# Moving two opening loads to other queues (f_logit's first block to ScalarE's, lower_bound to GpSimd's), and what is made from one of them to a later place

**Chip, cores, metric.** One core of one Trainium2 chip. The time is the device time of one execution in microseconds (us); lower is better. "Span" is the time from the first to the last instruction in the trace of one profiled execution.

## The reference

A gated recurrence over the sequence, then a two-layer block with g(h) = h - tanh(h):

```python
sig = 1.0 / (1.0 + np.exp(-f_logit))
f = lower_bound[None, None, :] + (1.0 - lower_bound[None, None, :]) * sig
i = 1.0 - f
for t in range(S):                      # S = 6080, B = 4, D = 256
    h = f[:, t] * h + i[:, t] * x[:, t]
    y[:, t] = h
h = y.reshape(B * S, D) @ w_in          # w_in 256 x 2048, w_out 2048 x 256
out = (h - np.tanh(h)) @ w_out          # weights arrive as float64
```

## The kernel before

The sequence is cut into blocks (block 0 has 256 tokens, the others 512). Every engine's instructions stand in a fixed order, written as words. The body is full of work for TensorE (PE); the change touches only the opening. There the words mean: `W.i` load weights i (raw float64, `W.0` and `W.1` are the halves of the first weights), `df.j`/`dx.j` load block j of f_logit/x, `tf`/`tx` transpose it on PE, `sg` sigmoid on ScalarE, `f0`/`f1` make the decay on ScalarE, `v0`/`v1` make the input on VectorE, `sc0`/`sc1` the scan on VectorE (its result is y), `ce cr cx cm cs cb cw` turn weights into float32 (`cr`, `cx` on ScalarE, the rest on VectorE), `F.j.u.s` a product of the first layer, `K1.n` 2n filler matmuls on zeros, which are meant to keep PE's clock up.

```python
before = """
    K1.7 df.0 ce.0 cr.0 dx.0 cm.0 tf.0 cx.0 W.1 cs.0 tx.0 sg0.0 cb.0 K1.4
    sg1.0 df.1 v0.0 f0.0 cw.0 f1.0 v1.0 dx.1 ce.1 tf.1 sc1.0 cx.1 sc0.0 W.2 cr.1
    cm.1 tx.1 sg1.1 cb.1 sg0.1 cs.1 F.0.0.0 f0.1 v1.1 f1.1 dx.2 v0.1 K1.4 cw.1
    t.0.0.0 sc0.1 q.0.0.0 F.0.0.1 w.0.0.0 W.3 sc1.1 cr.2 K1.2 a.0.0.0 t.0.0.1
    F.1.0.0 ...                                             # cut
"""
with tc.manual_schedule():
    nc.vector.memset(zeros[:], 0.0)
    nc.vector.memset(ones[:], 1.0)
    open_by(["W.0"])                    # one half on SyncE's queue, one on ScalarE's
    nc.scalar.dma_start(out=lb[:], in_=lower_bound.rearrange("(p k) -> p k", k=KC))
    make_identity(nc, ident[:])         # GpSimd; the transposes need it
    nc.scalar.activation(out=flag[:], in_=ones[0:1, :], func=AF.Sigmoid)
    nc.scalar.activation(out=om[:], in_=lb[:], func=AF.Identity, scale=-1.0, bias=1.0)
    nc.scalar.activation(out=nom[:], in_=lb[:], func=AF.Identity, bias=-1.0)
    busy = ps_b.tile([P, TB], FP32, name="B", tag="B")
    open_by(before.split())
    ...                                                     # cut: the body
```

## Time and profile before

| | before |
|---|---|
| time, median of 3 runs | 2330.19 us (2329.85 to 2331.65) |
| span of the profiled execution | 2328.7 us |
| PE / VectorE / ScalarE busy | 2319.0 / 2122.2 / 1802.3 us |
| PE idle before 11.92 us, after 2322.8 us, between | 3.84, 5.9, 0 us |

PE is never idle in the body, so the time is the opening, plus a body of fixed length, plus a tail. These lines of the timeline (start, duration, engine, line of the kernel, instruction; in brackets the idle time before it and what ended it) hold waits:

```profile
6.25 0.67 PE L673 MATMUL Qa<-ident,fn 128*128 128x128 f32 x2 [1.38 <-DMA fn<-in_f_logit_dram]
...
11.92 0.72 PE L673 MATMUL Qc<-ident,xn 128*128 128x128 f32 x4 [0.24 <-DVE e L160]
...
13.23 0.75 DVE L694 SCALAR_TENSOR_TENSOR v<-fT,om,Qd 128x512 f32<-128x512 f32 x1 [0.83 <-PE Qd L673]
```

The first is PE's first real work, the second the first transpose of x block 1, the third VectorE's first step on block 1, for which it idles 0.83 us. The list of issues (last column: us from issue to landing) has four of the five small loads of the opening (the other half of the weights, on SyncE's queue, is left out):

```profile
raw<-in_moe_w_in_dram ACTq DMA_DIRECT2D x1, 256.0 KB, 4.3
fn<-in_f_logit_dram SPq DMA_DIRECT2D x1, 256.0 KB, 4.7
xn<-in_x_dram SPq DMA_DIRECT2D x1, 256.0 KB, 4.9
lb<-in_lower_bound_dram ACTq DMA_DIRECT2D x1, 1.0 KB, 4.3
```

### The profile page before, as it was taken

To read this page: it belongs to the slowest core of one execution; us is meant where nothing else is said; L and a number is where in the kernel's file an instruction comes from. 1 tells how busy PE (TensorE), PEld (TensorE's weight loads), DVE (VectorE), ACT (ScalarE), POOL (GpSimd) and SP (SyncE) were. 2 spreads that over 40 slices of the span, in tenths; PEclk is the share of its full clock that TensorE was granted. 3 is DMA by queue.
4 is the path that set the end of the run, shared out by engine and by line. 5 is a ranking of instruction groups with operands and counts; after the bars stand their busy time and mean duration, and the time that the engine had idled before them with its cause. 6 is when DMAs were issued, how large, how long until landed. Compare 5 with 4: busy or idle time off the path is not lost.

```text
span 2328.7 us, 28694 instructions
## 1 busy us (share of the span) xinstructions
PE 2319.0 (100%) x10693; PEld 2027.1 (87%) x10693; DVE 2122.2 (91%) x2451; ACT 1802.3 (77%) x2688; POOL 0.7 (0%) x6
## 2 busy tenths in 40 slices
PE   9999999999999999999999999999999999999998
PEld 6888888888888888888888888888888888888887
DVE  8999899998999989999999999999899998999988
ACT  7677777777777777787777777777777777777775
POOL 0000000000000000000000000000000000000000
PEclk9999999999999999999999999999999999999999
DMA  6311211111111111112111121111211112111101
GB/s 172 64 23 33 41 37 28 28 37 37 37 28 28 38 36 37 28 28 42 32 37 28 28 45 29 37 28 28 45 29 37 28 28 46 31 34 28 28 10 28
DMA packets 296943, 85.00 MB, mean 37 GB/s; under 512 B 289888, under 2 KB 292704, under 8 KB 296800
## 3 DMA queue, kind: packets, MB, share of 16 engines
q1 hardware_dynamic: 296512, 82.87, 17.1%
q8 instruction: 84, 1.38, 0.3%
q14 instruction: 59, 0.48, 0.1%
q10 hardware_dynamic: 288, 0.26, 0.1%
HBM read 58.20 MB, written 24.90 MB: 36 GB/s over the span
## 4 chain that ended last, share of the span: by engine, by line
PE 99%; DVE 0%; DMA 0%; ACT 0%; issue 0%; ACTq 0%
PE A L392 27%; PE Qa L475 14%; PE Qb L475 14%; PE D L392 14%; PE Qd L475 14%; PE Qc L475 7%; PE B L392 7%; PE Qa L795 1%; PE Qc L795 1%; PE Qb L795 1%; PE A L728 1%; PE D L728 0%; PE Qd L728 0%; PE B L728 0%; DMA lb<-in_lower_bound_dram 0%; PE A L561 0%
## 5 line engine op out<-in xcount | busy, mean ns | idle before, releaser
L392 PE MATMUL A<-T,w_in 128*128 128x256 f32 x2208 | 558.8, 379 | 0.0
L392 PEld LDWEIGHTS A<-T,w_in 128*128 128x128 f32 x2208 | 419.5, 190 | 57.0
L436 DVE TENSOR_TENSOR h<-h,q 128x1024 f32<-128x1024 f32 x368 | 437.5, 1220 | 3.1
L430 DVE SCALAR_TENSOR_TENSOR q<-q,t 128x1024 f32<-128x1024 f32 x368 | 440.1, 1216 | 0.0
L423 ACT ACTIVATE q<-t 128x1024 f32<-128x1024 f32 x368 | 382.8, 1053 | 46.6 <-DVE h L436 43.7
L420 ACT ACTIVATE t<-h 128x1024 f32<-128x1024 f32 x368 | 388.7, 1057 | 3.1 <-DVE h L407 0.3
L441 ACT ACTIVATE junk<-t 128x1024 bf16<-128x1024 f32 x368 | 388.2, 1055 | 1.5
L455 DVE TENSOR_TENSOR Tg<-h 128x1024 f32<-128x1024 f32 x368 | 348.0, 946 | 6.4
L475 PE MATMUL Qb<-h,w_out 128*128 128x256 f32 x1472 | 347.7, 379 | 0.0
L475 PEld LDWEIGHTS Qb<-h,w_out 128*128 128x128 f32 x1472 | 279.7, 190 | 38.0
L475 PE MATMUL Qa<-Tg,w_out 128*128 128x256 f32 x736 | 219.0, 379 | 0.0
L475 PE MATMUL Qa<-h,w_out 128*128 128x256 f32 x736 | 218.9, 379 | 0.0
L475 PE MATMUL Qd<-h,w_out 128*128 128x256 f32 x732 | 217.7, 379 | 0.0
L475 PE MATMUL Qd<-Tg,w_out 128*128 128x256 f32 x732 | 217.7, 379 | 0.0
L404 ACT COPY h<-B 128x512 f32<-128x512 f32 x184 | 107.0, 582 | 142.8 <-PE B L392 94.1
L404 ACT COPY h<-A 128x512 f32<-128x512 f32 x184 | 107.1, 582 | 136.6 <-PE A L392 125.2
L407 DVE TENSOR_TENSOR h<-D,r 128x512 f32<-128x512 f32 x184 | 126.9, 689 | 92.7 <-PE D L392 89.1
L407 DVE TENSOR_TENSOR h<-A,r 128x512 f32<-128x512 f32 x184 | 126.3, 686 | 73.7 <-PE A L392 42.1
L404 ACT COPY r<-A 128x512 f32<-128x512 f32 x184 | 107.3, 583 | 105.7 <-PE A L392 105.7
L392 PE MATMUL D<-y,w_in 128*128 128x256 f32 x736 | 188.9, 379 | 0.0
L392 PE MATMUL B<-y,w_in 128*128 128x256 f32 x736 | 188.9, 379 | 0.0
L392 PE MATMUL A<-y,w_in 128*128 128x256 f32 x736 | 188.9, 379 | 0.0
(136 smaller groups left out, 3077.0 us busy)
## 6 DMA issues: line engine op xcount, KB each, us to landing
xn<-in_x_dram SPq DMA_DIRECT2D x184, 128.0 KB, 3.2
fn<-in_f_logit_dram SPq DMA_DIRECT2D x184, 128.0 KB, 3.1
out_dram<-osb SPq DMA_DIRECT2D x180, 128.0 KB, 2.8
raw<-in_moe_w_out_dram SPq DMA_DIRECT2D x8, 512.0 KB, 4.8
raw<-in_moe_w_in_dram SPq DMA_DIRECT2D x7, 512.0 KB, 5.2
out_dram<-osb SPq DMA_DIRECT2D x3, 256.0 KB, 3.9
fn<-in_f_logit_dram SPq DMA_DIRECT2D x1, 512.0 KB, 7.1
xn<-in_x_dram SPq DMA_DIRECT2D x1, 512.0 KB, 8.0
```

The costliest lines, as they stand in the source:

```text
L392: nc.tensor.matmul(ps[:, c], lhsT=w_in[u][:, slot, c * P : (c + 1) * P], rhs=mixes[j][right], start=start and c == 0, stop=True, skip_grou ...
L404: nc.scalar.copy(out=dst, in_=piece(n, bank))
L407: nc.vector.tensor_tensor(out=piece(n, "h")[:, q], in0=piece(n, bank), in1=piece(n, r), op=ALU.add)
L420: nc.scalar.activation(out=half(n, i, "t"), in_=half(n, i), func=AF.Square)
L423: nc.scalar.activation(out=half(n, i, "q"), in_=half(n, i, "t"), func=AF.Square, scale=RA, bias=RB,)
L430: nc.vector.scalar_tensor_tensor(out=q, in0=q, scalar=RC, in1=t, op0=ALU.add, op1=ALU.mult)
L436: nc.vector.tensor_tensor(out=h, in0=h, in1=q, op=ALU.mult)
L441: nc.scalar.activation(out=junk[:, :, :, 0 : st[n]["hb"]], in_=t, func=AF.Relu, bias=-TINY, accum_out=flags[:, 2 * n + i : 2 * n + i + 1],)
L455: nc.vector.tensor_tensor(out=o, in0=a, in1=b, op=ALU.subtract)
L475: nc.tensor.matmul(acc[j, part][:, r, 0 : st[n]["hb"]], lhsT=w_out[u][:, slot, c * P : (c + 1) * P], rhs=piece(n, right)[:, q, c], start=( ...
L728: nc.tensor.matmul(h[c], lhsT=w_in[u][:, 2 * k + s, c * P : (c + 1) * P], rhs=ys[j][:, k, 0:nb], start=k == 0 and (c == 0 or len(banks) == 2),
L795: nc.tensor.matmul(acc[j][i // 2][:, i % 2].rearrange("p (k m) -> p k m", k=2), lhsT=plain[j, u][:, s, c, i * P : (i + 1) * P], rhs=w_out[ ...
```

## The change

The intent: SyncE's queue issues six loads one after the other, so take one off it; and ScalarE waits for lower_bound (to make om and nom) before it may turn to the first weights, so load that elsewhere and make om and nom later.

```diff
-        def load(j, s):
+        def load(j, s, queue=nc.sync):
             nat = spot(j, ("fn", "xn")[s])
-            nc.sync.dma_start(
+            queue.dma_start(
 ...
-            K1.7 df.0 ce.0 cr.0 dx.0 cm.0 tf.0 cx.0 W.1 cs.0 tx.0 sg0.0 cb.0 K1.4
+            K1.7 ce.0 cr.0 dx.0 cm.0 tf.0 cx.0 L W.1 cs.0 tx.0 sg0.0 cb.0 K1.4
 ...
             open_by(["W.0"])
-            nc.scalar.dma_start(
+            nc.gpsimd.dma_start(
                 out=lb[:], in_=lower_bound.rearrange("(p k) -> p k", k=KC)
             )
+            load(0, 0, nc.scalar)
             make_identity(nc, ident[:])
 ...            # om and nom: from here into the word L, behind cx.0
```

## The prediction

> **What bounds the kernel now.** I read the page first. PE is busy for 2319.0 of 2328.7 us, at full granted clock:
>
> ```profile
> PE 2319.0 (100%) x10693; PEld 2027.1 (87%) x10693; DVE 2122.2 (91%) x2451; ACT 1802.3 (77%) x2688; POOL 0.7 (0%) x6
> PE   9999999999999999999999999999999999999998
> ```
>
> So 9.7 us of the span are idle on PE. I looked for them in the timeline. Before 12 us PE waits four times (1.70, 1.38, 0.52 and 0.24 us, together 3.84), and its last matmul ends at 2322.8, which leaves 5.9 us of tail. 3.84 + 5.9 is already 9.7: between 11.9 and 2322.8 us PE has no hole. What shifts PE's first real work shifts the end by the same amount, and what doesn't shift it is worth nothing. The change touches only the first microseconds, so the question is what releases PE at 11.92 us. Second view, the chain of waits followed back from the end, in its first 40 us:
>
> ```profile
> 1.41 4.25 DMA lb<-in_lower_bound_dram
> 5.69 0.03 ACT om L934
> 5.98 0.58 ACT r L146
> 6.59 0.69 DVE r L157
> ...
> 11.20 0.61 DVE e L160
> 11.92 0.72 PE Qc L673 x4
> 12.64 0.48 PE Qd L673 x4
> 13.12 1.73 PE A L728 x8
> ```
>
> This looks like an invitation: the chain begins with the 1 KB load of lower_bound, which the change takes away. But its step from "DVE e L160" to "PE Qc" is doubtful. In the program, that PE instruction (the first transpose of x block 1) waits for the DMA of x block 1 and for VectorE's earlier reads of bank Qc, not for e. So, third view, the transfers: the issue in the timeline (first two lines; start, duration), and time to landing in the list of issues.
>
> ```profile
> 3.15 0.59 SPq L659 DMA_DIRECT2D fn<-in_f_logit_dram  x1
> 3.78 0.53 SPq L659 DMA_DIRECT2D xn<-in_x_dram  x1
> 10.43 0.77 PE L673 MATMUL Qa<-ident,fn 128*128 128x128 f32 x4 [0.52 <-ACT e L149]
> ...
> fn<-in_f_logit_dram SPq DMA_DIRECT2D x1, 512.0 KB, 7.1
> xn<-in_x_dram SPq DMA_DIRECT2D x1, 512.0 KB, 8.0
> ```
>
> fn block 1 lands at 3.15 + 7.1 = 10.25, and PE starts its transposes at 10.43. xn block 1 lands at 3.78 + 8.0 = 11.78, and PE goes on at 11.92. Both releases are landings; the engines named merely ended at about the same time (e at 11.80). Fourth view, busy times by microsecond (last three columns: clock, DMA share, GB/s):
>
> ```profile
> 4.00:5.00 1.00, 0.87 (x5) 0.30 (x2) 0.00 (x0) 0.00 (x0) 0.00 (x0) 1.00 1.07 357
> 7.00:8.00 1.00, 1.00 (x7) 0.93 (x6) 0.99 (x3) 0.97 (x4) 0.00 (x0) 1.00 1.02 314
> 10.00:11.00 1.00, 0.57 (x4) 0.60 (x5) 1.00 (x3) 0.94 (x2) 0.00 (x0) 1.00 1.08 379
> ```
>
> The DMA engines are full from about 2.5 us until past the last packet of xn block 1. The opening is bound by bytes: 0.5 MB weights, 0.25 f, 0.25 x, 0.5 weights, 0.5 f, 0.5 x, together 2.5 MB, must have moved before PE can go on.
>
> **What the Trainium skill says.** "DMA: Bandwidth & Descriptors", section "Issuing engines are not separate DMA queues": transfers from SP, ACT and GpSimd run on the same 16 engines and interleave, so a second issuer saves only sequencer time. The trace agrees so far as it goes: each issue costs SP 0.4 to 0.66 us, while the engines are full. The same page, "Queues, rings and completion order": each DMA engine takes turns between the rings that hold work, packet by packet. In this trace, ACT's and SP's halves of the first weights end close together (landing 4.3 and 4.5 us after the same issue time, 0.99). The same page, "Specifications": about 1 us to the first byte by GpSimd's path against 0.6 by the others; no GpSimd transfer is in this trace. "TensorE: Matmul & The Clock Gate", Part 1: PE is cold at first and becomes fast after a busy window of some 3.4 us, free-running. The trace agrees in kind: block 0's transposes take 0.31 us each, block 1's 0.16.
>
> **The change, part by part.**
>
> 1. *SP's queue.* One issue of 0.44 us goes; those of xn 0, W.1, fn 1 and xn 1 start some 0.5 us earlier (xn 1 at about 3.3 in place of 3.78). Its packets then wait longer in a ring whose engines are full; bytes ahead of them are the same 2.0 MB. Landing of xn 1: 11.8 as before. Worth 0 (at most 0.1).
>
> 2. *fn 0 on ACT's queue.* Before, it went ahead of xn 0 in one ring: landings 1.45 + 4.7 = 6.15 and 1.94 + 4.9 = 6.84. Now the two are in two rings and share the engines by turns, so I expect both near 6.6 to 6.8: fn 0 some 0.5 us later, xn 0 unchanged. PE's first transposes begin at about 6.75 in place of 6.25, the first sigmoid at 7.45 in place of 6.97, the first v at 8.3 in place of 7.89. VectorE's run to the end of cs.1 moves from 12.40 to about 12.85. The next VectorE step, v of block 1, waits for PE until 13.23 (0.83 us idle before). So 0.45 is taken from a slack of 0.83: cost on the path 0.
>
> 3. *lower_bound on GpSimd's queue.* On ACT it landed at 1.41 + 4.25 = 5.66, because its tiny packets stood behind the weights. In a ring of its own it should land between 3 and 5. The identity, behind it on GpSimd, ends at 1.55 now and an estimated 1 us later, long before 6.2. Packets and bytes are about the same: 0.
>
> 4. *om and nom behind cx.* They held ACT from 5.69 to 5.89; without them r starts when the weights land, 5.57 as VectorE's e does: 0.3 us earlier. But ACT's sum until the sigmoid is the same, so at best it gains 0.1 there. VectorE's r starts at 6.35 in place of 6.59, e 0.25 earlier, w_in (8.29) with them or after v. The first product needs w_in, the scans (end 10.88) and x 1 transposed (13.12): the last decides. Off the path: 0.
>
> Sum: 0 from each, with at most 0.1 to 0.2 us of luck either way. 2330.19 becomes about 2330.0; the 0.2 is my allowance for the issues that come earlier.
>
> **Rivals.**
>
> A. *The chain is right and lower_bound is on the path.* Then r's 0.3 us go right through: 2329.9. For it: the chain view. Against it: the landing of xn 1 at 11.78, and 0.83 us of idle VectorE later, so VectorE can't have been the bound.
>
> B. *Earlier issue does bring earlier landing* (all SP transfers by up to 0.5 us). PE could then start block 1's transposes at 9.9 and lose its 0.52 and 0.24 idle: 2329.5. For it: the engines move only 154 GB/s in the microsecond from 2 to 3. Against it: that is latency on engines already occupied (share 0.94), not a lack of issued work.
>
> C. *Sharing delays fn 0 by over 0.9 us*, or lower_bound comes late (after 6.8). Then VectorE's slack is used up and the delay beyond it reaches the path: a few tenths, 2330.5.
>
> D. *The clock gate.* A later fn 0 lengthens PE's idle time from 1.38 to about 1.9 us. If the busy window is missed, the transposes and first products (some 2.5 us of work) run at half speed: up to 2 us, 2332. Against it: the filler matmuls that follow keep PE busy from 6.75 to 10.4, as now.
>
> **Range and chances.** The three runs of before span 1.8 us (2329.85 to 2331.65), which is more than each effect here; a median of three should move by some 0.7 to either side. I predict 2330.0 with 2328.9 to 2331.3: the lower end is B plus noise, the upper C or D in part. 2% would be 47 us, four times all that happens before PE starts. Chances: faster by over 2% 0.005, within 2% 0.99, slower 0.005.
>
> **What would show it.** Right: xn 1 lands within 0.2 of 11.8, PE's x-transposes start within 0.2 of 11.92, fn 0 lands later than 6.15, r starts about 5.57, VectorE still idles before v of block 1, and PE has no hole after 12 us. Wrong: the x-transposes start at 11.5 or earlier (A or B), or after 12.2, with a longer idle ended by something of block 0 (C), or block 1's transposes at 0.3 us each (D). A time outside the range with the first 12 us unmoved would mean that something in the body changed, for which I see no cause.

## The result, and the profile after

| | before | after |
|---|---|---|
| median of 6 runs each, same rounds | 2330.1 us (2328.41 to 2331.65) | 2329.64 us (2329.47 to 2330.7) |
| span of the profiled execution | 2328.7 | 2329.0 |

The ratio is 0.9999, 95% interval 0.9986 to 1.0011: the same. (Ratios here are the mean time of one kernel's fast runs over that of the other's of the same rounds, so not quite the ratio of the medians.)

The busy line of the page is unchanged but for PE, and the chain of waits of the kernel after now starts with f_logit's first block:

```profile
PE 2319.5 (100%) x10693; PEld 2028.2 (87%) x10693; DVE 2122.2 (91%) x2451; ACT 1802.4 (77%) x2688; POOL 1.4 (0%) x7
```

```profile
1.41 5.10 DMA fn<-in_f_logit_dram
...
8.61 1.71 PE B L900 x8
10.31 0.85 PE Qa L673 x4
11.17 0.85 PE Qb L673 x4
12.02 0.77 PE Qc L673 x4
12.79 0.46 PE Qd L673 x4
13.25 1.73 PE A L728 x8
```

The first product (A, last line) starts at 13.25 in place of 13.12 in this chain (its own records start at 13.09 and 12.96; starts of the first product below are of this second kind). But the way there is another one: PE no longer waits for block 1's data at all; from 6.65 on it is busy without a hole, with fillers (B) and with transposes that take 0.85 us for four where they took some 0.6. Why, the issues and the timeline of the kernel after show:

```profile
fn<-in_f_logit_dram SPq DMA_DIRECT2D x1, 512.0 KB, 7.1
xn<-in_x_dram SPq DMA_DIRECT2D x1, 512.0 KB, 8.0
fn<-in_f_logit_dram ACTq DMA_DIRECT2D x1, 256.0 KB, 5.1
xn<-in_x_dram SPq DMA_DIRECT2D x1, 256.0 KB, 4.8
lb<-in_lower_bound_dram POOLq DMA_DIRECT2D x1, 1.0 KB, 5.3
```

```profile
3.26 0.87 SPq L659 DMA_DIRECT2D xn<-in_x_dram  x1
...
5.34 0.68 ACT L146 ACTIVATE r<-raw 128x512 f32<-128x512 uint32 x1 [1.92 <-DMA raw<-in_moe_w_in_dram]
6.65 0.68 PE L673 MATMUL Qa<-ident,fn 128*128 128x128 f32 x2 [1.78 <-DMA fn<-in_f_logit_dram]
6.76 0.20 ACT L908 ACTIVATE om<-lb 128x2 f32<-128x2 f32 x1 [0.22 <-DMA lb<-in_lower_bound_dram]
8.30 0.48 DVE L694 SCALAR_TENSOR_TENSOR v<-fT,om,Qc 128x256 f32<-128x256 f32 x1 [0.80 <-PE Qc L673]
11.82 0.97 PE L673 MATMUL Qc<-ident,xn 128*128 128x128 f32 x4
13.36 0.75 DVE L694 SCALAR_TENSOR_TENSOR v<-fT,om,Qd 128x512 f32<-128x512 f32 x1 [0.55 <-PE Qd L673]
```

x block 1 landed at 3.26 + 8.0 = 11.23 (the landing itself is in the trace's semaphore records), 0.56 us earlier than in the trace of before. PE could not use it, for two reasons: block 0's transposes began 0.4 us later, so the eight fillers behind them ran until 10.3; and PE's clock, which the trace records as fast from 10.70 us on before, became fast only at 12.57 here. That looks like my rival B (earlier landing) and my rival D (late clock) at the same time, cancelling each other. Is that what the change does, or one execution's luck? That is what the experiments are for.

### The profile page after: what moved, and what is told of

It reads as the page before. It is cut to its first block, busy times and chain, and to the rows that moved or that the text cites. A ratio compares the mean times of both kernels' runs of the same rounds, so it can differ in the third digit from the quotient of the medians.

```text
span 2329.0 us, 28694 instructions
## 1 busy us (share of the span) xinstructions
PE 2319.5 (100%) x10693; PEld 2028.2 (87%) x10693; DVE 2122.2 (91%) x2451; ACT 1802.4 (77%) x2688; POOL 1.4 (0%) x7
## 4 chain that ended last, share of the span: by engine, by line
PE 99%; DMA 0%; DVE 0%; ACTq 0%; issue 0%
PE A L392 27%; PE Qa L475 14%; PE Qb L475 14%; PE D L392 14%; PE Qd L475 14%; PE B L392 7%; PE Qc L475 7%; PE Qb L795 1%; PE Qa L795 1%; PE Qc L795 1%; PE A L728 1%; PE D L728 0%; PE Qd L728 0%; PE B L728 0%; DMA fn<-in_f_logit_dram 0%; PE B L900 0%
## 5 line engine op out<-in xcount | busy, mean ns | idle before, releaser
L392 PE MATMUL D<-T,w_in 128*128 128x256 f32 x736 | 188.9, 379 | 0.0
```

The costliest lines, as they stand in the source:

```text
L392: nc.tensor.matmul(ps[:, c], lhsT=w_in[u][:, slot, c * P : (c + 1) * P], rhs=mixes[j][right], start=start and c == 0, stop=True, skip_grou ...
```

## The experiments

Two theories. **Theory 1**: the change really brings x block 1 earlier, and the late transposes and the cold clock give it back. **Theory 2** (first a rival, "luck", then a theory of its own): the landing and the clock's step differ from one execution to the next by more than the change moves them. The table has the trace of each kernel run, times in us from the start of the span. "Marker" is the start of the filler group between the second and the third product: what comes behind it is the same in all kernels. "Tail" is from the start of the last matmul to the landing of the last output.

| trace | x block 1 lands | clock fast | marker | tail | span |
|---|---|---|---|---|---|
| before | 11.79 | from 10.70 | 17.29 | 5.06 | 2328.7 |
| before_again | 11.22 | from 9.70 | 16.72 | 5.38 | 2328.4 |
| after | 11.23 | from 12.57 | 17.42 | 5.17 | 2329.0 |
| after_again | 11.67 | 4.61 to 11.44, from 14.85 | 18.53 | 5.04 | 2329.9 |
| fn_act | 11.37 | 4.82 to 11.65, from 15.06 | 18.47 | 5.04 | 2329.8 |
| lb_pool | 12.17 | from 13.74 | 18.36 | 4.95 | 2329.7 |
| bare | 11.52 | from 14.44 | 18.37 | 5.39 | 2330.1 |
| fill_before | 11.34 | from 4.47 | 16.84 | 4.15 | 2327.5 |
| fill_after | 11.67 | from 5.97 | 17.17 | 4.33 | 2327.9 |
| late_f | 12.29 | 6.22 to 9.64, from 13.05 | 20.49 | 4.14 | 2330.9 |
| late_f2 | 11.31 | from 6.22 | 18.46 | 4.13 | 2328.9 |
| place_fill | 11.98 | from 6.98 | 17.48 | 4.14 | 2327.9 |
| fill_before2 | 11.90 | from 7.19 | 17.40 | 4.32 | 2328.0 |
| fill_after2 | 11.23 | from 5.52 | 16.73 | 4.36 | 2327.5 |

The first four experiments ran on one chip, the eight others on a second; the kernel before had a median of 2330.8 to 2330.9 us on both. (Its runs are pooled by chip: nine for the first four experiments, nine for the next four, and the same nine with one more for the last four.)

Take the landing from the marker. In before, in before_again and in the five traces named fill or place_fill, what is left is 5.50 us: there the landing alone sets the marker. In after and lb_pool it is 6.19, in bare 6.85, in after_again 6.86 and in fn_act 7.10: this excess, 0.7 to 1.6 us, is what a late PE and a slow clock cost. (In late_f and late_f2 something else is in charge, see there.)

### before_again: the kernel before, unchanged

> The kernel before, unchanged, timed against itself. Theory 1 (two changes that cancel: with the change the transfers really land earlier, and PE loses it again to a late first transpose and a cold clock): x block 1 lands near 11.8 us again (11.6 to 12.0), and the DMA engines move 280 to 340 GB/s between 5.5 and 8.5 us again. Rival (the earlier landing in the trace after was luck of one execution): x block 1 lands anywhere from 11.2 to 11.8 here. Both: the ratio is 1.000, single runs spread over 1 to 3 us, and the time at which PE's clock becomes fast differs from the 10.70 us of the first trace by up to 3 us.

Measured: 2330.74 us (2329.41 to 2331.61) beside 2330.81 of the kernel before, ratio 1.0. x block 1 landed at 11.22, as early as in the trace after, without any change. Theory 1 wanted 11.6 to 12.0, and 280 to 340 GB/s between 5.5 and 8.5 us; it was 349 here, 300 in before. So the 0.56 us need not be an effect of the change: the unchanged kernel shows as much between two executions. The 16 DMA engines were about fully occupied in both traces (a share of 1.00 and 1.02), so a full share is not a fixed rate. The issues of before_again (512 KB lines, 6.6 and 7.4 in place of 7.1 and 8.0) say the same:

```profile
fn<-in_f_logit_dram SPq DMA_DIRECT2D x1, 512.0 KB, 6.6
xn<-in_x_dram SPq DMA_DIRECT2D x1, 512.0 KB, 7.4
```

### after_again: the changed kernel, unchanged

> The changed kernel, unchanged. Theory 1: x block 1 lands at 11.1 to 11.4 us again and 355 to 390 GB/s flow between 6 and 8.5 us. Rival: it lands anywhere from 11.2 to 11.8. Both: the ratio is between 0.9990 and 1.0005; f block 0 lands at 6.4 to 6.7 and lower_bound after 6 us; PE's clock becomes fast somewhere between 10 and 13.5 us, not at 12.57 as in the first trace, and the first product starts between 12.3 (fast early) and 13.3 (fast late).

Measured: 2330.71 us (2329.12 to 2331.48), ratio 0.9998. Here PE's clock did something that neither trace had shown. The timeline of after_again, PE alone:

```profile
7.25 0.40 PE L673 MATMUL Qd<-ident,xn 128*128 128x128 f32 x2
7.50 1.04 PE L900 MATMUL B<-zeros 128*128 128x256 bf16 x8
10.31 0.71 PE L673 MATMUL Qa<-ident,fn 128*128 128x128 f32 x4 [1.77 <-DMA fn<-in_f_logit_dram]
...
11.80 1.10 PE L673 MATMUL Qc<-ident,xn 128*128 128x128 f32 x4 [0.30 <-DMA xn<-in_x_dram]
12.70 1.06 PE L673 MATMUL Qd<-ident,xn 128*128 128x128 f32 x4
13.55 2.54 PE L728 MATMUL A<-y,w_in 128*128 128x256 f32 x8
```

The clock was fast early (the eight fillers took 1.04 us; 1.91 in the traces before and after). Therefore they ended early, PE idled 1.77 us, the clock fell at 11.44, and the first product ran at half speed: 2.54 us where it took 1.89. The clock column of the busy times by stretch (third from the end) shows the fall; the rows are 7 to 8, 11 to 12 and 13 to 14 us:

```profile
7.00:8.00 1.00, 1.00 (x11) 0.94 (x10) 0.66 (x3) 1.00 (x4) 0.00 (x0) 1.00 1.00 320
11.00:12.00 1.00, 0.69 (x6) 0.53 (x5) 1.00 (x2) 0.40 (x1) 0.00 (x0) 0.72 1.04 384
13.00:14.00 1.00, 1.00 (x6) 0.91 (x5) 0.13 (x1) 1.00 (x2) 0.00 (x0) 0.50 1.37 187
```

My expectation had the first product at 12.3 to 13.3 and the clock between 10 and 13.5; both missed. So did theory 1's 355 to 390 GB/s between 6 and 8.5 us (336) and its landing at 11.1 to 11.4 (11.67). In the table, every step of the clock within a trace is a multiple of 3.41 us from the next; where that grid lies differs between executions.

### fn_act: f_logit's block alone is moved

```diff
-            nc.gpsimd.dma_start(out=lb[:], ...)
             load(0, 0, nc.scalar)
+            nc.scalar.dma_start(out=lb[:], ...)
```

> The changed kernel, but lower_bound goes back to ScalarE's queue, behind f block 0. So f block 0 alone is moved. Theory 1, if the move of f is what makes the landings earlier: x block 1 lands at 11.1 to 11.4 us. If the move of lower_bound's 128 small packets is the cause: it lands near 11.8. Rival (luck): either, without pattern. lower_bound should land near 6 to 6.6 us. Ratio 0.9990 to 1.0010.

Measured: 2331.52 us (2329.48 to 2331.67), ratio 1.0002; x block 1 at 11.37, f block 0 already at 5.67, the clock fast at 4.82 and fallen at 11.65, as in after_again. lower_bound landed at 6.80, later than my 6 to 6.6. The landing of x block 1 fits the first theory's number, but lies within the spread of the unchanged kernel. (The edits of fn_act and lb_pool are against the changed kernel, those of bare, late_f and late_f2 against the kernel before or fill_before.)

### lb_pool: lower_bound alone is moved

```diff
-            K1.7 ce.0 cr.0 dx.0 ... cx.0 L W.1 ...
+            K1.7 df.0 ce.0 cr.0 dx.0 ... cx.0 L W.1 ...
-            load(0, 0, nc.scalar)
```

> The changed kernel, but f block 0 goes back to SyncE's queue. So lower_bound alone is moved (and what is made from it stands behind the first weights' steps). Theory 1 with f as the cause: x block 1 lands near 11.8 us and f block 0 at 6.1; with lower_bound's packets as the cause: 11.1 to 11.4. lower_bound lands at 6 to 7 us as in the trace after, if GpSimd's queue as such is late, or at 3 to 5 if it was two busy rings that held it. Ratio 0.9990 to 1.0010.

Measured: 2330.77 us (2330.22 to 2331.23), ratio 1.0. x block 1 landed at 12.17, the latest of the first six traces, and f block 0 at 5.38. lower_bound landed at 1.48 + 4.1 = 5.6, neither at my 3 to 5 nor at 6 to 7. Neither part of the change moves the time by more than its spread.

### fill_before and fill_after: enough fillers to hold the clock

If the clock causes the spread, more fillers should narrow it.

```diff
-            K1.7 ...  sg0.0 cb.0 K1.4
+            K1.12 ... sg0.0 cb.0 K1.10
```

> The kernel before with 24 filler matmuls in place of 14 ahead of block 0's transposes, and 20 in place of 8 behind them. Theory 2 (the spread between executions comes from where PE's clock steps fall, in a grid of 3.41 us, and from the landing of x block 1): PE has no idle stretch over 1 us after 1.7, so the clock becomes fast between 5.1 and 8.6 us and stays fast; PE goes on within 0.2 us of each landing; the first product starts 1.0 to 1.2 us after x block 1 has landed, at 12.3 to 13.2 us; span = that start + 2315.7 (from the traces so far). Ratio 0.9994 to 0.9999, and the single runs lie within 1 us of each other where the kernel before spreads over 2 to 3. Rival (the clock is no part of it): same as before, first product at 12.4 to 14 as until now, same spread.

> The changed kernel with the same fillers. Theory 2: as fill_before, the same time as it within 0.4 us (the change moves no landing of x block 1); a consistent gain of 0.4 us or more over fill_before would say that the change does bring x block 1 earlier and the clock had hidden it.

Measured: fill_before 2329.59 us (2328.99 to 2329.97), fill_after 2329.32 (2328.5 to 2329.42), the kernel before on the same chip 2330.91 (2328.94 to 2331.61); ratios 0.9995 and 0.9992, both intervals with 1 inside. The spread fell from 2.7 us (nine runs) to 1.0 and 0.9 (five runs each), and the clock stayed fast from 4.47 (just before my 5.1 to 8.6) and 5.97 us on. In the later call, below, the spreads were 1.5 and 1.3: still narrower, but less so. The timeline of fill_before, PE alone, shows cleanly what the prediction had read in the trace of before, that both releases of PE are landings:

```profile
6.99 2.35 PE L899 MATMUL B<-zeros 128*128 128x256 bf16 x20
10.03 0.72 PE L673 MATMUL Qa<-ident,fn 128*128 128x128 f32 x4 [0.70 <-DMA fn<-in_f_logit_dram]
11.47 0.72 PE L673 MATMUL Qc<-ident,xn 128*128 128x128 f32 x4 [0.24 <-DMA xn<-in_x_dram]
12.51 1.89 PE L728 MATMUL A<-y,w_in 128*128 128x256 f32 x8
```

The first product starts 1.17 us after x block 1's landing in both traces (11.34 and 12.51; 11.67 and 12.84). But my span formula (that start + 2315.7) gives 2328.2 for fill_before, and the span was 2327.5. The difference is not in the body: from the start of the last filler to the start of the last matmul it is 2304.91 to 2305.07 us in all fourteen traces. It is in the tail. With the old number of matmuls a fetch of instructions falls beside the last output transfers; with the fillers it doesn't. The transfers at the end, first of before (from 2322 us on), then of fill_before, from 2321 us on (queue, packets, MB, share; then the last outputs, last column us to landing):

```profile
q1 hardware_dynamic: 544, 0.52, 19.5%
q8 instruction: 1, 0.02, 1.2%
...
out_dram<-osb SPq DMA_DIRECT2D x2, 256.0 KB, 4.0
```

```profile
q1 hardware_dynamic: 544, 0.52, 17.2%
q14 instruction: 3, 0.02, 0.8%
...
out_dram<-osb SPq DMA_DIRECT2D x2, 256.0 KB, 2.8
```

The q8 line, one packet of 16 KB, is gone: it starts 1.4 to 2.3 us after the last matmul in the seven traces with the old number of fillers or fewer, and 6.0 to 6.2 us before it in the seven with more. Their tails are 4.95 to 5.39 and 4.13 to 4.36 us. So about 0.9 of the 1.3 us that the fillers gain in the medians is the tail, and not the clock. That the fetch is what slows the outputs is not shown but inferred: the two go together in all fourteen traces, and no run moved the fetch alone. (That the fetch is PE's is inferred too: only PE's instruction count differs.)

### bare: the fillers taken away

```diff
-            K1.7 df.0 ... cb.0 K1.4
+            K1.1 df.0 ... cb.0
```

> The kernel before with its fillers ahead of the first product taken away but for two. Theory 2: the clock becomes fast only after 3.4 us of PE work from 10.3 us on, at 13.4 to 17 us; block 1's transposes take 0.21 us or more each (start to start), the first product runs at half speed for part; the second filler group behind it starts at 18 to 20 us in place of 16.7 to 18.5, and the time is 0.5 to 2 us over the kernel before. Rival (fillers don't matter, the landing decides): the same time as before.

Measured: 2331.4 us (2330.89 to 2332.31) beside 2330.91, ratio 1.0003; clock fast at 14.44, marker 18.37, the first product (from 13.64 on) partly at half speed, 2.29 us, all as expected; the time, 0.49 us over, is just under my low edge of 0.5. Single executions with the old fillers can be no better off than this: after_again, fn_act and lb_pool had their marker at 18.4 to 18.5. The two traces of the kernel before had not (17.29 and 16.72), but four of its nine runs took 2331.26 us or more.

### late_f and late_f2: how much slack has VectorE?

The prediction let f block 0 come later because VectorE idled before block 1. Here it comes much later, behind the second weights.

```diff
-            K1.12 df.0 ce.0 cr.0 dx.0 cm.0 tf.0 cx.0 W.1 cs.0 tx.0 ... K1.10
+            K1.12 ce.0 cr.0 dx.0 cm.0 W.1 df.0 tf.0 cx.0 cs.0 tx.0 ... K1.10     # late_f
+            K1.24 ce.0 cr.0 dx.0 cm.0 W.1 df.0 tf.0 cx.0 cs.0 tx.0 ...           # late_f2
```

> fill_before with f block 0 loaded behind the second half of the first weights, so it lands about 2.3 us later (8.2 to 8.8 in place of 6.1). My prediction gave VectorE 0.83 us of slack there. Theory: 2.1 us later minus 0.8 of slack, so 1.0 to 1.5 us over fill_before, the group of filler matmuls behind the second product starting that much later, and no VectorE idle before v of block 1. Rival (VectorE's work on block 0 has more slack than I read): under 0.5 us.

Measured: 2332.7 us (2332.47 to 2333.3), 3.1 over fill_before. A miss by construction: f landed at 9.30 (8.2 to 8.8 expected), PE idled 2.75 us until then, its clock fell (9.64 to 13.05), and the 20 fillers behind block 0 kept block 1's transposes waiting until 14.24. VectorE still idled 0.92 us before block 1. It says nothing about VectorE's slack.

> A cleaner late_f: f block 0 again behind the second half of the first weights (landing near 9.3 us, VectorE's first v near 10.2 in place of 7.3), but 48 filler matmuls ahead of block 0's transposes and none behind them, so that no filler stands between block 0 and block 1. Theory: VectorE's chain from that v is 2.9 us later, less 0.97 us of idle that it has in fill_before, so about 1.9 us over fill_before, VectorE without idle before v of block 1, the second filler group behind the second product near 18.7 us. Rival (more slack than read): the first product 1.0 to 1.2 us after x block 1's landing and the time within 0.6 us of fill_before plus what x block 1 lands later.

Measured: 2330.58 us (2330.44 to 2330.91), 1.06 over fill_before2; marker 18.46. f block 0 landed at 8.39 (near 9.3 expected), but the 48 fillers held PE until 9.14, so they, and not the load, set the delay: VectorE's first v moved from 7.29 in fill_before to 10.14, by 2.85, and its idle time was used up; v of block 1 moved from 12.78 to 14.57, by 1.79. That is 2.85 less the 0.97 that fill_before idled, within 0.1. PE now waits for VectorE, not for a landing (timeline of late_f2, PE):

```profile
13.19 1.99 PE L728 MATMUL A<-y,w_in 128*128 128x256 f32 x8 [0.55 <-DVE y L235]
16.63 1.99 PE L728 MATMUL A<-y,w_in 128*128 128x256 f32 x8 [0.58 <-DVE w_in L136]
```

The slack is read rightly; 1.9 us was too much for the medians, because fill_before's other executions have later landings (11.90 in fill_before2) and so less to lose (this is argued, not tested). With no landing in charge, the four runs lie within 0.5 us.

### place_fill, fill_before2, fill_after2: is lower_bound on the path, and has the change a gain of its own?

place_fill is fill_before with om and nom behind cx (the word `L`) and nothing else.

> fill_before with om and nom behind cx and nothing else of the change. Rival A of the prediction (lower_bound's landing is on the path): ScalarE's r starts 0.3 us earlier and the time falls by 0.3 us against fill_before2. My theory: r starts when the weights have landed, VectorE's idle before v of block 1 grows or stays at 0.5 to 1.2 us, the first product still starts 1.0 to 1.2 us after x block 1's landing, and the median is within 0.3 us of fill_before2 in either direction.

> fill_before once more, to be compared with place_fill and fill_after2 on the same chip. Median 0.7 to 1.6 us below the kernel before, single runs within 1.2 us of each other.

> fill_after once more. Theory 2: median within 0.4 us of fill_before2, spread within 1.2 us, both below the kernel before by 0.7 to 1.6 us; f block 0 and x block 0 land together again and later than in fill_before2. If the change does have a gain of its own that the clock hides, fill_after2 is again below fill_before2, by 0.3 us or more.

Measured, same chip: place_fill 2329.35 us (2328.71 to 2329.88), fill_before2 2329.52 (2329.18 to 2330.7), fill_after2 2328.81 (2328.45 to 2329.78). Ratios to the kernel before 0.9994, 0.9995, 0.9992, each interval with 1 inside. In place_fill ScalarE's r no longer waits for lower_bound: it starts at 5.36, with VectorE's e at 5.37 (5.89 and 5.57 in fill_before2):

```profile
5.36 0.68 ACT L146 ACTIVATE r<-raw 128x512 f32<-128x512 uint32 x1 [1.97 <-DMA raw<-in_moe_w_in_dram]
...
7.31 0.39 ACT L687 ACTIVATE fT<-Qa 128x256 f32<-128x256 f32 x1 [0.56 <-PE Qa L673]
```

The gain ends as 0.56 us of idle ScalarE before the first sigmoid, and VectorE's idle before block 1 is 1.03 us (0.61 in fill_before2). The first product started 1.16 us after x block 1's landing, as in the other kernels. So lower_bound was not on the path. The medians differ by 0.17 us, inside the spread. (The fillers held block 0's transposes until 6.80 in both kernels, 0.9 and 0.7 us after f had landed, so this shows it for the kernel with fillers; for the kernel before it rests on VectorE's 0.83 us of idle time.)

My expectations missed here more than once: fill_before2 and fill_after2 spread over 1.5 and 1.3 us (1.2 expected), fill_after2 lies 2.0 us below the kernel before (0.7 to 1.6 expected), and 0.71 below fill_before2, where theory 2 allowed 0.4 and I had set 0.3 or more as the sign of a gain of the change's own.

The change on top of fillers gave 0.27 us in the first call and 0.71 in the second. Pooled, the ten runs of the changed kernel have a mean 0.59 us below the eleven of the other; a simple 95% interval for two samples is 0.2 to 1.0. In the traces, x block 1 lands at 11.23 to 11.67 (mean 11.43 of five) where f block 0 is on ScalarE's queue, and at 11.22 to 12.17 (mean 11.70 of seven, late_f and late_f2 left out) where it is on SyncE's. Both hint at rival B in a small size, but the ranges of the landings overlap, and 0.3 us of landing is not 0.6 us of time; it stays open. So does a weak form of theory 1: without fillers three of three traces with f block 0 on ScalarE's queue lost 0.7 to 1.6 us to a late PE and a slow clock, and one of three with it on SyncE's queue (0.7 us). Six traces can't tell this from chance.

## Why the prediction was right, point by point

The measured 2329.64 us lies 0.4 from the 2330.0 predicted, with single runs 1 to 3 us apart: so close a number says little, and the steps below count for more. One of them was luck: the transposes of x block 1 started at 11.82, inside the 0.2 us around 11.92 that I had set as a sign of being right, but because PE was late from its fillers and slow, while the landing that was to release them had come at 11.23.

- **What sets the end.** Right: opening, rigid body, tail. The body is the same to 0.16 us in all traces, and PE has no hole in it.
- **What releases PE at 11.92.** Right: x block 1's landing. fill_before and fill_after start the first product 1.17 us after it, and the marker follows it by 5.50 us in seven traces; place_fill shows that lower_bound, first in the chain view, is off the path. The name "DVE e" there was of an engine that had ended at about the same time.
- **Part 1, SyncE's queue: worth 0.** The issue came 0.52 us earlier, as said. The landing at "11.8 as before" was too exact: 11.22 to 12.17 with f on SyncE's queue. I had one trace and took its landing for a constant. In the trace after it was 11.23, outside my 0.2. Whether the worth is 0 or some tenths is not settled (the 0.59 us above).
- **Part 2, fn 0 later into VectorE's slack.** Right nearly step by step in the trace after: f at 6.52 (6.6 to 6.8 said), PE at 6.65 (6.75), first v at 8.30 (8.3), cs.1's end at 12.82 (12.85), 0.55 us of idle left. late_f2 confirms the slack. xn 0 was not "unchanged": it landed at 6.2 in place of 6.8, after an issue 0.49 us earlier. And the 0.4 us had a second effect that I had filed under the clock only: the fillers behind end later, at 10.3, after block 1's f had landed (9.73).
- **Part 3, lower_bound "between 3 and 5".** Wrong: 6.73, later than the 5.66 of before. The reason given (its packets stood behind the weights' in one ring) fails too: in lb_pool, alone in its ring, it landed at 5.6. ScalarE even waited 0.22 us for it. It did no harm because ScalarE then idled 0.31 us for PE before the first sigmoid (7.37); an estimate from these lines is that a landing later by more than that would have begun to delay the sigmoid.
- **Part 4, om and nom.** Right: r started as soon as the weights had landed (5.34), and the gain was lost in front of the sigmoid.
- **Rival D** was right as a mechanism; that the change causes it is not shown. The clock's step falls anywhere from 4.6 to 15.1 us in the kernels with the old fillers (9.70 and 10.70 in the two traces of the unchanged one), and lb_pool, with f block 0 where it was, lost 0.7 us too. Of the spread of 2 to 3 us that I took for noise without a cause, the traces show two parts: this one (0 to 1.6 us) and the landing (0.95 us from the earliest to the latest). The 0.31 and 0.16 us that I gave for one transpose are lengths of groups, divided; from start to start it is 0.21 us in the slow state and 0.12 in the fast one.

## What to carry to other kernels

When one engine is never idle in the body, look only for what releases its first and last work, and read that from landings and from the program's waits; the engine named in a chain of waits may just have ended at the same time. Before reading a cause out of half a microsecond between two traces, take the same kernel's trace again: here repeats differed by 0.6 us in the landing and by 8 in the clock's first step (after: 12.57 and 4.61). A change of the number of fillers came with another tail here (0.9 us shorter), so compare opening, body and tail apart and not only totals.

## What the Trainium skill lacked or had wrong

- "TensorE: Matmul & The Clock Gate", Part 1: the free-running window is confirmed (steps 3.41 or 6.83 us apart). It gives the way down as after at least one idle window; here the clock fell after windows in which PE was still busy for 48% (after_again, 8.03 to 11.44) and 39% (fn_act), and held through one with 52% (after_again, 4.61 to 8.03). It rose after windows with 81% (fill_before) and more, not after 78% (lb_pool, 3.50 to 6.92). The shares are worked out from the idle times in the timelines, where PE's ends are modelled, so the last per cents are rough.
- Same page, Part 4 (PE-mode transpose), says that the fast state doesn't engage for transposes. In these traces FP32 transposes start every 0.21 us in the slow state and every 0.12 in the fast one, and in lb_pool the clock rose at 13.74 after a window (10.33 to 13.74) in which PE ran transposes alone, for 86% of it. (The trace names them MATMUL; it does not say whether they use the page's transpose mode.)
- "DMA: Bandwidth & Descriptors", Specifications: about 1 us to the first byte from GpSimd. In the trace after, lower_bound was issued from 1.48 to 2.15 us and its first packet moved at 5.10, with two other rings busy. The section "Issuing engines are not separate DMA queues" fits as far as the runs can tell: x block 1 was issued 0.52 us earlier, and no single call shows a gain clear of the spread (pooled, with fillers, 0.59 us, open).
- "Runtime: NRT & Kernel Launch", Instruction fetch mechanics, calls the cost of a 16 KiB boundary mostly hidden. Here the last outputs landed 0.9 us later in the seven traces where one such fetch, 16 KB, ran beside them than in the seven where it had run before; that the fetch is the cause is inferred.
